# Sharing a weight copy between VectorE and GpSimd, and placing two ScalarE output copies ahead of a sigmoid, in a fused retention and mixture-of-adapters kernel

## The chip, the cores and the metric

The kernel runs on one core of a Trainium2 chip. The metric is the device time of one execution in microseconds (us). A core has TensorE (PE, matmuls; PEld is its weight load), VectorE (DVE), ScalarE (ACT), GpSimd (POOL) and SyncE (SP, which here issues most DMA transfers). Each engine runs its own instructions in program order and waits on semaphores for the others.

## The reference

A retention layer (attention with a decay instead of a softmax) feeds a mixture of low-rank adapters. With B = 8, H = 8, S = 576 and head size 64:

```python
scores = scale * np.matmul(q, k.transpose(0, 1, 3, 2))
Dmat = np.where(rel >= 0, gamma[:, None, None] ** rel[None, :, :], 0.0)   # rel = i - j
ret = scores * Dmat[None]
attn_out = np.matmul(ret, v)
x = attn_out.transpose(0, 2, 1, 3).reshape(B * S, H * D)                  # 4608 x 512

logits = x @ w_gate                                                       # 8 adapters
topk = the 2 adapters with the largest logits;  w = softmax over these two
delta = sum over the two of  w * ((x @ A[e]) @ B[e])                      # rank 16
out = x + delta
```

## The kernel before, in words

The decay factorizes, so the sequence is cut in chunks of 128 positions (four full ones and a last one of 64). A *unit* is one chunk of two batch entries, with all 8 heads; a *quad* is one chunk of four entries, and it is loaded as a whole: q, k and v by one transfer each from SP (`issue`, line 225). There are 18 units; units 0 to 3 are the first chunk.

For each unit t the kernel goes through stages, all called by hand in the loop at the end of the function:
- `stage_T`: q and k are transposed on TensorE into PSUM (tiles pqT, pkT) and copied to SBUF (qT, kT). For each name there are two banks g = 0 and 1. With `shared=True` the copy of g = 1 is VectorE's and that of g = 0 ScalarE's; otherwise both are ScalarE's, but for the q of units 0 and 1, which are VectorE's.
- `stage_S`: scores (ps) per head pair, multiplied by the mask on VectorE (rt). `scale_k` on GpSimd multiplies k by decay factors; `stage_U` forms the state update (pu).
- `stage_Q` and `stage_R`: the old state and the masked scores give the retention output (px), which VectorE scales into xT, one tile per batch entry g.
- `stage_Z`: for both g, TensorE multiplies xT by AW[g], which holds the adapters' A (columns 0 to 127, `ER`) and the gate (columns 128 to 135), giving pz. Then VectorE copies the logits (lg), takes their maxima (m) and a bias ns. `stage_V` is the sigmoid of the routing on ScalarE (sg), and `stage_W` forms the routing weights (cm) and the weighted low-rank activations (zc) on VectorE.
- `stage_B` transposes xT back into the output banks po[cc], `stage_X` transposes zc (pzt, then zT on ScalarE), and `stage_Y` adds zT times B (`Bcat`) to po (`mm_Y`), copies the four pieces of po to SBUF (osb, `copy_Y`: cc chooses the bank, g the half of it) and stores them from SP (`store_Y`).

Units have their heads on the partitions in one order for g = 0 and with the partition halves exchanged for g = 1. So AW is needed twice: AW[0], and AW[1], which is AW[0] with its two halves of 64 partitions exchanged. `place_A` puts A into AW[0] by matmuls (pa) and four ScalarE copies; a GpSimd transfer (line 679) brings the gate. Lines 693 and 694 are the two GpSimd copies from AW[0] to AW[1], and line 695 is the GpSimd transfer of B.

What sets the order: TensorE, VectorE and ScalarE instructions are recorded through `mm`, `vec` and `act` (lines 81, 84, 87), which chain every instruction of an engine to the one before it, so each of these engines runs in the order in which the stages are called; `chain("pool", ...)` does the same for a few GpSimd instructions. So all TensorE matmuls have line 81, all chained VectorE operations line 84 and all ScalarE operations line 87; tiles, not lines, tell them apart. The eight PSUM banks are handed out from a first-in first-out list: `bank` takes the oldest free one, `done` appends a bank when its last reader has been recorded. A tile that gets a bank waits for the last reader of the tile that had it before. In this way the two banks of unit 3's pkT are one that the pzt of unit 0 left, and the bank of po[0] of unit 0.

The stretch that the diff touches is the body of `t == 0`: units 0 and 1, with the transposes of units 2 and 3 already begun. `stage_Y(0, copies=("act", "dve"))` gives the two pieces of bank cc = 0 to ScalarE and those of cc = 1 to VectorE.

Of the kernel before, what the change touches and what calls it, by code (L numbers as in the profile page):

```python
# [18 lines left out]
def kernel(  # L19
# [15 lines left out]
    ER = E * R  # L35
# [21 lines left out]
    for hp in range(HP):  # L57
        for ho in range(2):
            g = gam[2 * hp + ho]
# [13 lines left out]
    def chain(eng, i):  # L73

        i = getattr(i, "ins", i)
        if eng in queued:
            tc.add_manual_dep(i, queued[eng].name, order, reason="program order")
        queued[eng] = i
# [4 lines left out]
    def vec(fn, **kw):  # L83
        chain("dve", getattr(nc.vector, fn)(**kw))  # L84
# [31 lines left out]
    gp = nc.gpsimd  # L116
# [3 lines left out]
    for base in (0, -L):  # L120
        gp.affine_select(
            out=id64, in_=id64, compare_op=ALU.not_equal, fill=1.0, base=base,
# [129 lines left out]
    def rows(g):  # L252
        return slice(64 * g, 64 * g + 64)
# [17 lines left out]
    def stage_T(t, names=("qT", "kT"), shared=False):  # L271

        s = st.setdefault(t, {})
        for nm in names:
            src = nat[units[t]][0 if nm == "qT" else 1]
            dst = s[nm] = wk.tile([128, 2, HP, C], FP32, tag=nm, name=nm, bufs=4 if nm == "qT" else 2)
            ps = [bank([128, HP, 2, L], f"p{nm}") for _ in range(2)]
            for hp in range(HP):
                for b in range(2):
                    for g in range(2):  # L280
                        mm(
                            ps[g][:, hp, b, :],
                            lhsT=src[rows(g), b, 2 * hp : 2 * hp + 2, :],
                            rhs=id64[rows(g), :],
                            is_transpose=True,
                            start=True,
                            stop=True,
                        )
            for g in range(2):
                if is_full(t):  # L290
                    o = dst[:, :, :, rows(g)].rearrange("p b a i -> p a b i")
                else:
                    o = dst[:, g].rearrange("p a (b i) -> p a b i", b=2)
                if t < 2 and nm == "qT" or shared and g == 1:
                    vec("tensor_copy", out=o, in_=ps[g])
                else:
                    act("copy", out=o, in_=ps[g])
            done(*ps)
# [214 lines left out]
    def stage_Z(t, gs=BOTH):  # L513

        s = st[t]
        n = len(gs)
        pz = bank([128, n, ER + E], "pz")
        for y, g in enumerate(gs):
            for dt in range(HP):
                mm(  # L520
                    pz[:, y, :],
                    lhsT=s["xT"][g][:, dt, :],
                    rhs=AW[g][:, dt, :],
                    start=(dt == 0),
                    stop=(dt == HP - 1),
                    skip_group_check=True,
                )
        m8 = mo.tile([128, n, E], FP32, tag=f"m8{n}", name="m8")
        ns = mo.tile([128, n], FP32, tag=f"ns{n}", name="ns")
        lg = mo.tile([128, n, E], FP32, tag=f"lg{n}", name="lg")  # L530
        if n == 2:
            vec("tensor_copy", out=lg, in_=pz[:, :, ER : ER + E])
        else:
            lg = pz[:, :, ER : ER + E]
        for y in range(n):
            vec("max", out=m8[:, y, :], in_=lg[:, y, :])
        vec(
            "scalar_tensor_tensor",
            out=ns, in0=m8[:, :, 0], scalar=-1.0, in1=m8[:, :, 1],
            op0=ALU.mult, op1=ALU.subtract,  # L540
        )
        s[("route", gs)] = lg, m8, ns, pz

    def stage_V(t, gs=BOTH):
        s = st[t]
        n = len(gs)
        lg, m8, ns, pz = s[("route", gs)]
        sg = mo.tile([128, n, E], FP32, tag=f"sg{n}", name="sg")
        for y in range(n):
            act(  # L550
                "activation",
                out=sg[:, y, :], in_=lg[:, y, :], func=AFT.Sigmoid,
                bias=ns[:, y : y + 1], scale=2.0,
            )
        s[("route", gs)] += (sg,)
# [26 lines left out]
    def mm_Y(t, gs=BOTH):  # L582

        s = st[t]
        if gs[0] == 0:
            s["osb"] = outp.tile([128, 2, HP, 2, Dh], FP32, tag="osb", name="osb")
        bv = Bcat.rearrange("p (a o d) -> p a o d", a=HP, o=2)
        for cc in range(2):
            for g in gs:
                mm(  # L590
                    s["po"][(cc, g)],
                    lhsT=s["zT"][g],
                    rhs=bv[:, :, cc ^ g, :],
                    start=False,
                    stop=True,
                    skip_group_check=True,
                )
# [26 lines left out]
    def stage_Y(t, gs=BOTH, copies=("act", "act")):  # L624

        mm_Y(t, gs)
        for cc in range(2):
            for g in gs:
                copy_Y(t, cc, g, copies[cc])
        store_Y(t, gs)  # L630
# [40 lines left out]
    for t in range(NU):  # L671
        if units[t][2] == 0:
            issue(quads.index(units[t][:2]) + 2, (0, 1, 2) if t <= LATE else (0,))
        if t == 0:
            spin(10)
            first_T()
            scale_k(0)
            fill_pick(3)
            gp.dma_start(
                out=AW[0][:, :, ER : ER + E], in_=moe_w_gate.rearrange("(t p) e -> p t e", p=128)  # L680
            )
            for ho in range(2):
                act("copy", out=asc[1][rows(ho)], in_=asc[0][rows(1 - ho)])
            act(
                "copy", out=gdec.rearrange("p a b d -> p a (b d)"),
                in_=gde.unsqueeze(2).broadcast_to((128, HP, 2 * Dh)),
            )
            stage_S(0)
            stage_U(0)
            stage_Q(0)  # L690
            stage_R(0)
            place_A()
            for ho in range(2):
                chain("pool", gp.tensor_copy(out=AW[1][rows(ho)], in_=AW[0][rows(1 - ho)]))
            chain("pool", gp.dma_start(out=Bcat, in_=moe_B.rearrange("e r d -> (e r) d")))
            stage_T(1, ("qT",))
            stage_T(1, ("kT",), shared=True)
            scale_k(1)
            stage_Z(0)
            stage_S(1)  # L700
            stage_W(0)
            stage_U(1)
            stage_Q(1)
            stage_R(1)
            stage_T(2, ("qT",))
            stage_B(0)
            stage_X([0])
            stage_Z(1)
            stage_V(1)
            stage_Y(0, copies=("act", "dve"))  # L710
            stage_T(2, ("kT",), shared=True)
            stage_T(3)
            scale_k(2)
            scale_k(3)
            stage_S(2)
            stage_W(1)
            stage_S(3)
            for u in (2, 3):
                stage_U(u)
                stage_Q(u)  # L720
                stage_R(u)
            late_T(4)
            for ho in range(2):
                gp.tensor_tensor(
                    out=maskh[ho], in0=trih.unsqueeze(1).broadcast_to((128, HP, L)),
                    in1=heads(1, ho, L), op=ALU.mult,
                )
            continue
        if t < 4 or units[t][2] or not is_full(t):
            continue  # L730

        before, near = [u for u in (t - 4, t - 3) if u > 0], (t - 2, t - 1)
        here = (t, t + 1)
        for u in here:
            for b, nm in enumerate(("qT", "kT")):
                stage_S(u, (b,))
                if t > LATE:
                    stage_T(u + 2, (nm,))
            if t > LATE:
                scale_k(u + 2)  # L740
        for u in before:
            stage_B(u)
        stage_X(before)
        stage_Z(near[0])
        stage_V(near[0])
        for u in before:
            stage_Y(u)
        stage_Z(near[1])
        stage_V(near[1])
        if t > LATE:  # L750
            issue(t // 2 + 2, (1,))
        if units[t][0] > 0:
            for u in here:
                stage_Q(u)
        for u in near:
            stage_W(u)
        for u in here:
            if t > LATE and u == here[1]:
                issue(t // 2 + 2, (2,))
            stage_U(u)  # L760
            if units[t][0] == 0:
                stage_Q(u)
            stage_R(u)
        if t <= LATE:
            late_T(t + 2)
# [80 lines left out]
```

## Time and profile before

| | |
|---|---|
| median of 4 runs | 184.32 us (183.04 to 186.62) |
| the profiled execution's own time | 183.96 us |
| its span, first to last instruction | 182.3 us |
| granted TensorE clock, mean | 0.991 |
| busy: PE, DVE, ACT, POOL | 173.9, 114.7, 67.0, 58.6 us |
| HBM traffic | 28.91 MB read, 9.44 MB written |

The profile is one execution as the hardware profiler took it. Times count from the start of the span. A timeline row reads: start, duration (from the first to the end of the last of a merged group), engine, line, operation, output tile, input tiles, shape, count, and in brackets how long the engine had been idle before it and what ended that wait. The chain of waits is followed back from the last instruction, at each step to what released it. A wait on several semaphores is put down to the one that came last by the profile. Matmuls are pipelined, so the duration of one is longer than the distance between two.

### The profile page before, as it was taken

The page shows a single profiled execution, that of the slowest core. Times are in us where ns is not written, and L with a number is a line of the kernel's source. Part 1 is how long each engine was busy: PE and PEld are TensorE (multiplying, and loading weights), DVE is VectorE, ACT ScalarE, POOL GpSimd, SP SyncE. Part 2 cuts the span into 40 slices and gives each one's busy share as a digit, 9 for nine tenths or more (in the row PEclk, how much of TensorE's full clock was granted, in tenths as well). Part 3 has the DMA queues.
Part 4 walks back from the last instruction along what each step waited for, and adds up shares of the span by engine and source line. Part 5 has one row for each costly group of instructions (what it writes and reads, how often), then busy time and mean ns, then how long its engine had stood idle before and what let it go on. Part 6 is the DMA issues. An engine that isn't in the chain of part 4 may idle for free.

```text
span 182.3 us, 8097 instructions
## 1 busy us (share of the span) xinstructions
PE 173.9 (95%) x3606; PEld 162.6 (89%) x3606; DVE 114.7 (63%) x293; ACT 67.0 (37%) x180; POOL 58.6 (32%) x69
## 2 busy tenths in 40 slices
PE   7897999999999999999999999999999999999980
PEld 2596989999999999999999999999999999999970
DVE  3594856988567836866267816792488446557471
ACT  3512127043313243197602753075505460031461
POOL 8865208044026500687022710444050003200000
PEclk9999999999999999999999999999999999999996
DMA  6998979999798898769898989997691041014055
GB/s 138 278 229 210 318 211 297 274 288 278 213 284 247 245 320 233 217 192 294 230 327 286 297 248 313 262 201 154 236 203 29 4 177 60 4 57 182 7 229 230
DMA packets 53219, 38.74 MB, mean 213 GB/s; under 512 B 26928, under 2 KB 48576, under 8 KB 53184
## 3 DMA queue, kind: packets, MB, share of 16 engines
q1 hardware_dynamic: 50784, 37.49, 71.3%
q10 hardware_dynamic: 2224, 0.58, 1.5%
q8 instruction: 28, 0.46, 1.1%
q0 software_dynamic: 176, 0.15, 0.5%
q14 instruction: 7, 0.06, 0.1%
HBM read 28.91 MB, written 9.44 MB: 210 GB/s over the span
## 4 chain that ended last, share of the span: by engine, by line
PE 91%; DMA 3%; DVE 2%; ACT 1%; ACTq 1%; issue 0%
PE px L81 24%; PE pz L81 19%; PE ps L81 17%; PE pu L81 9%; PE po L81 9%; PE pkT L81 5%; PE pqT L81 5%; DMA k<-in_k_dram 3%; PE pzt L81 2%; PE pe L81 1%; DVE qT L84 1%; ACT osb L87 1%; PE pa L81 1%; ACT sg L87 0%; ACTq L225 0%
## 5 line engine op out<-in xcount | busy, mean ns | idle before, releaser
L84 DVE TENSOR_TENSOR rt<-ps,mask 128x512 f32<-128x512 f32 x64 | 40.3, 685 | 8.9 <-PE ps L81 8.0
L264 POOL TENSOR_TENSOR k<-k,pack 128x512 f32<-128x512 f32 x32 | 32.6, 1044 | 25.1 <-PE pkT L81 18.4
L423 POOL TENSOR_TENSOR P<-pn,gdec 128x512 f32<-128x512 f32 x12 | 15.3, 1277 | 68.2 <-DVE pn L84 64.0
L81 PE MATMUL pz<-AW,xT 128*128 128x136 f32 x288 | 37.1, 282 | 0.0
L81 PEld LDWEIGHTS pz<-AW,xT 128*128 128x128 f32 x288 | 34.6, 190 | 0.2
L81 PE MATMUL ps<-qT,kT 64*128 64x128 f32 x512 | 34.1, 278 | 0.0
L81 PEld LDWEIGHTS ps<-qT,kT 64*128 64x128 f32 x512 | 30.7, 188 | 1.2 <-issue 0.8
L81 PE MATMUL px<-rt,v 128*64 128x128 f32 x512 | 30.7, 273 | 0.0
L87 ACT COPY qT<-pqT 128x512 f32<-128x512 f32 (+1 forms) x33 | 16.8, 568 | 31.3 <-PE pqT L81 31.3
L81 PEld LDWEIGHTS px<-rt,v 128*64 128x64 f32 x512 | 27.7, 137 | 0.0
L84 DVE TENSOR_TENSOR xT<-px,asc 128x512 f32<-128x512 f32 x36 | 24.4, 689 | 4.0 <-PE px L81 2.6
L87 ACT COPY kT<-pkT 128x512 f32<-128x512 f32 x29 | 16.0, 600 | 27.4 <-PE pkT L81 18.7
L84 DVE COPY lg<-pz 128x16 f32<-128x16 f32 x17 | 3.0, 175 | 32.5 <-PE pz L81 32.5
L87 ACT COPY osb<-po 128x256 f32<-128x256 f32 x59 | 17.3, 388 | 2.7 <-PE po L81 2.0
L81 PE MATMUL pu<-v,k 128*64 128x64 f32 x512 | 18.1, 224 | 0.0
L81 PEld LDWEIGHTS pu<-v,k 128*64 128x64 f32 x512 | 16.6, 138 | 1.4 <-issue 1.0
L87 ACT ACTIVATE sg<-lg,ns 128x8 f32<-128x8 f32 x34 | 8.4, 294 | 23.3 <-DVE ns L84 22.9
L81 PE MATMUL pkT<-id,k 64*128 64x64 f32 x288 | 12.7, 225 | 1.8 <-DVE qT L84 1.3
L81 PE MATMUL px<-qT,P 64*64 64x128 f32 (+1 forms) x512 | 14.2, 259 | 0.0
L81 PEld LDWEIGHTS pkT<-id,k 64*128 64x128 f32 x288 | 11.2, 139 | 2.9 <-DVE qT L84 1.5
L84 DVE TENSOR_TENSOR pn<-pu,P 128x512 f32<-128x512 f32 x12 | 8.3, 692 | 8.3 <-PE pu L81 8.3
L81 PEld LDWEIGHTS px<-qT,P 64*64 64x64 f32 x512 | 12.6, 133 | 0.9
(59 smaller groups left out, 149.6 us busy)
## 6 DMA issues: line engine op xcount, KB each, us to landing
out_dram<-osb SPq DMA_DIRECT2D x36, 256.0 KB, 3.9
v<-in_v_dram SPq DMA_DIRECT2D x4, 512.0 KB, 7.2
q<-in_q_dram SPq DMA_DIRECT2D x3, 512.0 KB, 5.3
k<-in_k_dram SPq DMA_DIRECT2D x3, 512.0 KB, 7.6
q<-in_q_dram SPq DMA_DIRECT2D x2, 256.0 KB, 4.2
k<-in_k_dram ACTq DMA_DIRECT2D x2, 256.0 KB, 4.8
Arow<-in_moe_A_dram SPq DMA_DIRECT2D x1, 256.0 KB, 6.8
Bcat<-in_moe_B_dram POOLq DMA_DIRECT2D x1, 128.0 KB, 4.7
```

The costliest lines, as they stand in the source:

```text
L81: chain("pe", nc.tensor.matmul(*args, **kw))
L84: chain("dve", getattr(nc.vector, fn)(**kw))
L87: chain("act", getattr(nc.scalar, fn)(**kw))
L264: gp.tensor_tensor(out=kk[:, b], in0=kk[:, b], in1=gv[:, 0].unsqueeze(2).broadcast_to((128, H, Dh)), op=ALU.mult,)
L423: nc.gpsimd.tensor_tensor(out=Pt, in0=pn, in1=gdec, op=ALU.mult)
```

## The change

The two parts lie in the body of `t == 0`. The first gives the A columns of one half of AW[1] to VectorE, behind the q copies of unit 1, and leaves GpSimd that half's gate columns (64 partitions x 4 x 8). The second takes `stage_Y(0)` apart and calls it ahead of `stage_V(1)`: ScalarE's two osb copies of unit 0 come before unit 1's sigmoid pair. The order of TensorE's and of SP's instructions stays as it was; VectorE's order gains one copy, GpSimd's second AW copy is smaller, and ScalarE's order differs in those four instructions.

```diff
             place_A()
-            for ho in range(2):
-                chain("pool", gp.tensor_copy(out=AW[1][rows(ho)], in_=AW[0][rows(1 - ho)]))
+            chain("pool", gp.tensor_copy(out=AW[1][rows(0)], in_=AW[0][rows(1)]))
+            chain("pool", gp.tensor_copy(out=AW[1][rows(1), :, ER:], in_=AW[0][rows(0), :, ER:]))
             chain("pool", gp.dma_start(out=Bcat, in_=moe_B.rearrange("e r d -> (e r) d")))
             stage_T(1, ("qT",))
+            vec("tensor_copy", out=AW[1][rows(1), :, 0:ER], in_=AW[0][rows(0), :, 0:ER])
             stage_T(1, ("kT",), shared=True)
             scale_k(1)
             stage_Z(0)
...
             stage_B(0)
             stage_X([0])
             stage_Z(1)
+            mm_Y(0)
+            for cc, eng in enumerate(("act", "dve")):
+                for g in range(2):
+                    copy_Y(0, cc, g, eng)
+            store_Y(0)
             stage_V(1)
-            stage_Y(0, copies=("act", "dve"))
             stage_T(2, ("kT",), shared=True)
             stage_T(3)
             scale_k(2)
```

## The prediction

> **What bounds the kernel now.** I read the page's busy shares first, then its 40 slices, then the whole chain of waits in order of time, and then, for the two places that the diff touches (13 to 20 us and 25 to 31 us), the timeline of each engine.
>
> ```profile
> PE 173.9 (95%) x3606; PEld 162.6 (89%) x3606; DVE 114.7 (63%) x293; ACT 67.0 (37%) x180; POOL 58.6 (32%) x69
> PE   7897999999999999999999999999999999999980
> PEclk9999999999999999999999999999999999999996
> ```
>
> TensorE is busy 95% of the span at the full granted clock until the last slice. An edit to another engine can only pay where TensorE stands still, and all its idle time is 182.3 - 173.9 = 8.4 us, start and tail included. So the first question is which of its idle time the edits can reach. The chain of waits around the two places:
>
> ```profile
> 13.81 0.69 PE pqT L81 x16
> 14.50 1.29 DVE qT L84 x2
> 15.79 0.01 issue
> 15.80 0.71 PE pkT L81 x16
> 16.51 2.05 PE pz L81 x16
> 18.56 1.99 PE ps L81 x32
> ...
> 27.36 0.49 ACT sg L87 x2
> 27.85 0.54 ACT osb L87 x2
> 28.39 0.04 issue
> 28.44 0.71 PE pkT L81 x15
> 29.15 3.78 PE ps L81 x64
> ```
>
> There are two holes. The first, 14.50 to 15.80, is put down to VectorE's qT copies. That name cannot be right: pkT reads k and writes the two banks that the xT products left, and those products were done before the qT copies began. The other thing pkT needs is the second k load, issued at 7.92 us; the trace's answer for k between 7.5 and 9.5 us is
>
> ```profile
> DMA to landing us min/median/max: 7.7/7.7/7.7
> ```
>
> and 7.92 + 7.7 = 15.6 us, just ahead of pkT's first weight load at 15.77. The hole is a transfer's, and the diff does not touch that transfer. The second hole, at 28.4, is ScalarE's. The weight loads and ScalarE's own row there:
>
> ```profile
> 28.01 0.14 PEld L81 LDWEIGHTS pkT<-id,k 64*128 64x128 f32 x1
> 28.43 0.57 PEld L81 LDWEIGHTS pkT<-id,k 64*128 64x128 f32 x15 [0.28 <-ACT osb L87]
> 28.92 2.70 PEld L81 LDWEIGHTS ps<-qT,kT 64*128 64x128 f32 x44
> ```
> ```profile
> 27.36 0.49 ACT L87 ACTIVATE sg<-lg,ns 128x8 f32<-128x8 f32 x2 [1.96 <-DVE ns L84]
> 27.76 0.62 ACT L87 COPY osb<-po 128x256 f32<-128x256 f32 x2
> 28.28 0.59 ACT L87 COPY kT<-pkT 128x512 f32<-128x512 f32 x1
> 28.75 1.09 ACT L87 COPY qT<-pqT 128x512 f32<-128x512 f32 x2
> 29.71 1.11 ACT L87 COPY kT<-pkT 128x512 f32<-128x512 f32 x2
> ```
>
> Unit 3's kT transposes write two banks. The first was free; the second is the bank of the first output's half cc = 0, which ScalarE frees with its second osb copy at 27.76 + 0.62 = 28.38. In the timeline these 16 transposes take 1.08 us where the 16 of unit 2 just before take 0.71: the hole costs 0.37 us. ScalarE stood idle for 1.96 us ahead of the sigmoid, in program order, while the osb copies behind it had their data.
>
> **Part 1, the weight copies.** Before: two GpSimd copies of 64x544 (15.43 to 16.74; 636 ns each). After: one of them stays; GpSimd's second shrinks to 64x32; VectorE takes 64x512, behind its qT copies (end 14.49 + 1.29 = 15.78) and ahead of its kT copy (16.55).
>
> GpSimd's small copy: the nearest rows are 64x64 at 239 ns and a 128x1 memset at 100 ns; I take 0.24, so GpSimd ends near 16.07 + 0.24 = 16.3 instead of 16.74. VectorE's copy: no row copies SBUF to SBUF there. Its copy of 512 elements from PSUM takes 0.69, its memset of 256 words 0.27; bounds 0.27 and 0.69. I take 0.69, the row with the same element count, which ends at 15.78 + 0.69 = 16.47, inside the 0.78 us for which VectorE idles before kT.
>
> Who reads the result: stage_Z(0), whose first eight matmuls use AW[0] and whose last eight use AW[1]. It starts at 16.44, behind the transposes of unit 1, and half of its 2.05 us brings it to AW[1] near 17.4. The copies were there at 16.74, 0.7 us early; now they are there at 16.5. TensorE waited for neither in the trace and gains nothing. The same holds for what is queued behind on GpSimd: the Bcat load moves from 16.69 to about 16.3 (it landed 4.7 us after its issue, 21.4, and its first reader runs at 26.48), and scale_k(1) from 17.35 to about 17.0 (its reader, stage_U(1), starts at 20.48). On VectorE the kT copy and the routing's lg wait for TensorE in any case (0.78 and 1.35 us idle before them). SP's queue keeps its order. Term: 0. The cover is about 0.7 us of early arrival; past it, each 0.1 us of lateness costs 0.1 us.
>
> [...]
>
> [...] With the three copies strictly one after another, GpSimd 15.43 to 16.07, VectorE to 16.76, GpSimd to 17.00: still 0.4 us ahead of 17.4. The kT copy would then run 16.76 to 17.45, against its reader S(1) at 18.49. So the first part costs 0 to its upper bound as well. Nothing excludes a small loss from a slower copy than any row shows; that is the slower rival below.
>
> **Part 2, the osb copies ahead of the sigmoid.** The matmuls of po and their order are unchanged: stage_Y's matmuls already stood ahead of unit 2's transposes on TensorE. ScalarE's first osb copy waits for two of the four po matmuls; these start 0.11 us apart from 26.48 and the last ends at 27.08, so the second ends at 26.86. ScalarE has been free since 25.40. The two copies run 26.90 to 27.52 (0.62 for the pair). The sigmoid's bias ns is ready at 27.17 + 0.16 = 27.33, so the sigmoid pair now starts at 27.5 instead of 27.36 and ends at about 27.98 instead of 27.85: 0.13 later. Its first reader, cm of stage_W(1), ran at 32.52: hidden by 4.5 us. VectorE's own osb copies wait for the last po matmul as before. The output's two stores are issued from SP in the same place of its queue, at 35.88 behind a v load, so copies that end 0.9 us earlier do not move them.
>
> Behind the sigmoid on ScalarE, unit 2's kT copy starts 0.4 us earlier, since ScalarE now works in what was idle time: about 27.88 to 28.47 instead of 28.28 to 28.87. The copies after it follow, and the last kT copy of unit 3 ends near 30.82 - 0.39 = 30.43.
>
> TensorE: the bank is free at 27.52, before the transposes reach it at 28.07, so 0.37 us of stall go. What is late next? S(2), which began its weight loads at 28.92, needs kT of unit 2 from both engines. ScalarE's half is there at 28.47. VectorE's half is not moved by the diff: 27.91 + 0.68 = 28.59, and with the 0.05 us that lay between ScalarE's half (28.87) and S(2) it can start at 28.64. The gain is 28.92 - 28.64 = 0.28 us; bounds 0 and 0.37. I take 0.28, because VectorE's chain lg, m, ns, osb, osb, kT is unchanged row by row.
>
> Does it last? S(3) begins half of the two units' 3.78 us after S(2), at about 30.55, and ScalarE's last kT copy ends at 30.43, so it does not hold it. From 30.11 to 40.5 VectorE works without a break, but that run starts with a product that waits 1.52 us for S(2), so it shifts along. The third quad's k load, issued at 28.24 with 9.1 us to landing, is there at 37.3, and its transposes would come at 38.37 - 0.28 = 38.09. After 41 us the transfers land microseconds ahead. So 0.28 us should reach the end.
>
> **Sum.** The profiled execution took 183.96 us around a span of 182.3: 183.96 - 0 - 0.28 = 183.68, span 182.0. It lies 0.36 us under the median of the four runs, 184.32; against that median the forecast is 184.32 - 0.28 = 184.0 us. A measurement of this kernel can tell about 1% (1.8 us) from no change, so the verdict should be "the same".
>
> **Rivals.**
> - *The gain is given back (184.3).* Place: the third quad's k load. It lands 0.8 us before the earlier transposes. DMA runs at 0.94 of its engines in that stretch, and a landing 0.8 to 1.1 us later than in this execution takes all of it. For it: the four runs differ by 2%. Against it: the profiled margin.
> - *Slower: the weight copies run late.* Mechanism: VectorE and GpSimd slow each other on their concurrent copies. It decides from an end past 17.4. If all three are serial and each takes twice its row: 15.43 + 1.27 + 1.38 + 0.48 = 18.56, 1.2 us late, and 184.32 + 1.2 - 0.28 = 185.2. For it: the three are now on two engines at one moment. Against it: before, GpSimd's copies took 634 and 637 ns although VectorE's qT copy ran beside the first.
> - *The edit does nothing (184.3).* It would be so if the osb copies, now in front, had to wait for po past 27.36. The po matmuls end by 27.08, and Bcat has landed 5 us before: little for it.
>
> **How the numbers follow.** The forecast, a gain of 0.2 to 0.37: 60%. Gain given back or never there: 24%. Late copies: 8%. Something that no row shows: 8%, either way. Nearly all of the first two, and a late copy of 1.2 us, lie within 1%. So: within 1% 0.86, slower 0.08, faster 0.06. The range reaches up to the late copies, 185.2. Below, no part gives more than 0.37, but the runs of one kernel scatter more than that: I reach to the fastest run of before, 183.0. The likeliest case's own range is 183.9 to 184.1 around that median.
>
> **What would show it.** Right: in the changed profile the wait of pkT's weight load on ACT osb near 28.4 is gone; osb stands at about 26.9 and the sigmoid after it; the transposes of unit 3 take about 0.7 us; S(2) starts at about 28.64, then waiting for VectorE's kT; the hole at 14.5 to 15.8 is as it was. Wrong: pz waits for VectorE or GpSimd near 17.4; or pkT at 38 waits for its load; or an earlier S(2) without a shorter span.

## The result and the profile after

| | before | after |
|---|---|---|
| median of the runs, us | 184.41 (182.93 to 188.09) | 184.54 (182.65 to 187.23) |
| the profiled execution, us | 183.96 | 182.65 |
| its span, us | 182.3 | 181.0 |

The ratio after to before is 0.9998 (95% interval 0.9978 to 1.0018): no difference that this measurement can tell. (The ratio leaves out executions more than 1.5% above the kernel's fastest, so it is not quite the ratio of the two medians.) A second measurement of the same kernel on another occasion, among the experiments below, gave 0.9942 (0.9901 to 0.9984). The forecast was 183.68/183.96 = 0.9985: well inside the first interval, just above the second, whose own ratio would be a gain of 1.1 us. The two intervals share only 0.9978 to 0.9984. The times alone do not settle whether 0.28 us were won; for that the traces are needed.

The page of the changed kernel, its span and busy times:

```profile
span 181.0 us, 8099 instructions
PE 173.9 (96%) x3606; PEld 162.4 (90%) x3606; DVE 115.2 (64%) x294; ACT 67.1 (37%) x180; POOL 58.1 (32%) x69
```

TensorE does the same 173.9 us of work in a span 1.3 us shorter. Most of that is not the change's. The chain of waits (start, length, what):

```profile
7.70 7.04 DMA k<-in_k_dram
14.73 0.14 issue
14.87 0.71 PE pkT L81 x16
15.58 2.05 PE pz L81 x16
17.63 1.99 PE ps L81 x32
...
26.80 0.51 PE pqT L81 x16
27.31 0.51 PE pkT L81 x16
27.81 1.14 PE ps L81 x16
```

Unit 1's transposes now begin at 14.87 instead of 15.80, and here the chain names the releaser: the k load, landed at 14.73. In this execution it simply landed 0.93 us earlier. So hole and load go together, and an execution's time contains this load's luck. The second place, in the weight loads of TensorE and then in ScalarE's rows:

```profile
27.09 0.59 PEld L81 LDWEIGHTS pkT<-id,k 64*128 64x128 f32 x16
27.78 3.68 PEld L81 LDWEIGHTS ps<-qT,kT 64*128 64x128 f32 x64
```
```profile
25.98 0.65 ACT L87 COPY osb<-po 128x256 f32<-128x256 f32 x2 [1.50 <-PE po L81]
26.51 0.51 ACT L87 ACTIVATE sg<-lg,ns 128x8 f32<-128x8 f32 x2
26.90 0.59 ACT L87 COPY kT<-pkT 128x512 f32<-128x512 f32 x1
```

Unit 3's transposes are one group of 16 again, with no wait on osb in it; osb runs while ScalarE would wait for ns, and the sigmoid follows. To take the first load's luck out, count from the first weight load of S(1) to the first weight load of later groups (S(t) and U(t) are `stage_S` and `stage_U` of unit t):

| S(1) to, us | S(2) | U(2) | S(4) | third quad's k load lands before its reader by |
|---|---|---|---|---|
| before | 10.43 | 14.37 | 22.14 | 0.99 |
| after | 10.22 | 14.02 | 21.85 | 0.28 |

So 0.21 us are won at S(2), 0.35 at U(2) and 0.29 at S(4). From S(1) to the end of the span it is 163.4 instead of 163.8 us.

### The profile page after: what moved, and what is told of

Its sections match the earlier page's. It is cut to its first block, busy times and chain, and to the rows that moved or that the text cites. A ratio compares the mean times of both kernels' runs of the same rounds, so it can differ in the third digit from the quotient of the medians.

```text
span 181.0 us, 8099 instructions
## 1 busy us (share of the span) xinstructions
PE 173.9 (96%) x3606; PEld 162.4 (90%) x3606; DVE 115.2 (64%) x294; ACT 67.1 (37%) x180; POOL 58.1 (32%) x69
## 4 chain that ended last, share of the span: by engine, by line
PE 83%; issue 5%; DMA 4%; SPq 4%; ACT 2%; DVE 1%; ACTq 0%
PE px L81 21%; PE pz L81 19%; PE ps L81 15%; PE po L81 9%; PE pu L81 7%; PE pkT L81 4%; PE pqT L81 4%; DMA k<-in_k_dram 4%; SPq L171 2%; PE pzt L81 2%; SPq L225 2%; PE pe L81 1%; ACT kT L87 1%; ACT qT L87 1%; ACT osb L87 0%
## 5 line engine op out<-in xcount | busy, mean ns | idle before, releaser
L87 ACT COPY kT<-pkT 128x512 f32<-128x512 f32 x29 | 16.0, 600 | 26.5 <-PE pkT L81 17.7
L81 PE MATMUL px<-qT,P 64*64 64x128 f32 (+1 forms) x512 | 14.1, 259 | 0.0
L87 ACT COPY zT<-pzt 128x512 f16<-128x512 f16 (+2 forms) x12 | 5.8, 483 | 18.9 <-PE pzt L81 18.9
```

The lines of the kernel that those rows point to most:

```text
L81: chain("pe", nc.tensor.matmul(*args, **kw))
L87: chain("act", getattr(nc.scalar, fn)(**kw))
```

## The experiments

The table gives those whose stretches can be compared, all counted as above; the others follow in the text. "pkT to S(1)" counts from unit 1's k transposes and is the stretch in which the weight copies are used; the two landings are those of unit 1's k load and the third quad's.

| kernel | ratio to before (95%) | first landing | third quad's | pkT to S(1) | S(1) to S(2) | to U(2) | to S(4) |
|---|---|---|---|---|---|---|---|
| before | | 15.66 | 37.38 | 2.72 | 10.43 | 14.37 | 22.14 |
| full change | 0.9998 (0.9978 to 1.0018) | 14.73 | 36.80 | 2.72 | 10.22 | 14.02 | 21.85 |
| full again | 0.9942 (0.9901 to 0.9984) | 14.51 | 36.83 | 2.78 | 10.22 | 14.02 | 21.86 |
| part 1 alone | 1.0002 (0.9968 to 1.0036) | 15.15 | 39.13 | 2.74 | 10.49 | 14.42 | 23.49 |
| part 2 alone | 0.9976 (0.9944 to 1.0008) | 14.34 | 36.80 | 2.73 | 10.32 | 14.12 | 21.99 |
| late osb, half | 0.9993 (0.9944 to 1.0041) | 14.91 | 38.10 | 2.73 | 11.00 | 14.84 | 22.72 |
| slow copies | 1.0115 (1.0070 to 1.0159) | 15.87 | 38.83 | 3.78 | 10.21 | 14.02 | 21.84 |
| q first, full | 0.9951 (0.9905 to 0.9997) | 14.50 | 37.65 | 2.73 | 10.21 | 14.01 | 22.09 |
| both q first | 0.9996 (0.9949 to 1.0043) | 14.32 | 38.24 | 3.16 | 10.22 | 14.02 | 22.42 |

**Part 2 alone.** The hunk of the diff around `mm_Y(0)`, without the one around `place_A()`.

> Only the output copies move ahead of the sigmoid; the weight copies are as before. Theory (TensorE-bound, the bank wait at 28.4 us goes, 0.28 us reach the end): the wait of the second pkT weight load on osb is gone; measured from the first weight load of unit 1's pkT (which follows the k load's landing), S(2) comes 0.2 to 0.28 us earlier than before, S(3) up to 0.38, everything after 41 us 0.28; ratio near 0.9985, hardly to be told from 1. Rival 1 (the gain is given back at the third quad's k load): the same up to 31 us, but unit 4's pkT waits for its load, and the distance from unit 1's pkT to S(4) is that of before. Rival 2 (the weight copies cost what the output copies bring): a ratio clearly below that of the full change, about 0.997.

The wait on osb is gone. S(2) comes 0.11 earlier than before, U(2) 0.25, S(4) 0.15. That is the gain of the full change less 0.1, and at S(2) less than the expected 0.2: between 17 and 23 us TensorE lost 0.1 us in this execution, which has nothing to do with osb, and at 36.9 the third quad's load (landed 36.80) left no margin. Ratio 0.9976 with an interval that holds 1: as expected, not to be told from it, so it does not decide rival 2 either.

**Part 1 alone.** The hunk around `place_A()`, without the other.

> Only the weight copies are shared; the output copies are as before. Theory: no distance between TensorE's groups changes by more than 0.03 us; pz starts when pkT ends and does not wait for VectorE or GpSimd; ratio 1.000. Rival 2: pz's second half waits for VectorE's copy, 0.1 us or more; ratio about 1.0015 or above.

Nothing is won and nothing lost up to U(2) beyond 0.06, and the ratio, with a third of a per cent either way, shows no cost. But its profile shows the first rival at work, by a transfer that neither part touches (TensorE's rows):

```profile
36.31 1.70 PE L81 MATMUL px<-rt,v 128*64 128x128 f32 x28
39.26 0.71 PE L81 MATMUL pkT<-id,k 64*128 64x64 f32 x16 [1.26 <-DMA k<-in_k_dram]
```

The third quad's k load landed at 39.13 and TensorE stood still for 1.26 us. In such an execution any gain ahead of it is given back. What moves this landing is mostly when SP issues the load: over all profiles between 27.09 (the copies made to meet) and 29.71 us (slow copies), here at 29.70; from issue to landing it is 8.7 to 9.5 us everywhere.

**The output copies late.** On the kernel before, ScalarE's two copies go behind three other copies of ScalarE's:

```diff
             stage_V(1)
-            stage_Y(0, copies=("act", "dve"))
+            mm_Y(0)
+            for g in range(2):
+                copy_Y(0, 1, g, "dve")
+            done(*st[0]["banks"].values())
+            st[0]["banks"] = {}
             stage_T(2, ("kT",), shared=True)
-            stage_T(3)
+            stage_T(3, ("qT",))
+            for g in range(2):
+                copy_Y(0, 0, g, "act")
+            store_Y(0)
+            stage_T(3, ("kT",))
```

> The opposite of part 2, made large: on the kernel before, ScalarE's two output copies of unit 0 go behind the copies of unit 2's kT and unit 3's qT. The bank of unit 3's second pkT half is then free near 29.9 instead of 28.4. Theory (what is lost or won at 28 us reaches the end): the wait grows from 0.36 to about 1.85 us, S(2) comes 1.5 later, S(3) 1.3 to 1.5 later, and the time rises by about 1.35 us, ratio 1.007. Rival 1 (time at 28 us is absorbed by the wait for the third quad's load at 37 to 38 us): S(2) as late, but S(4) less than 0.7 us late; ratio 1.000 to 1.003.

Ratio 1.0081 (1.0042 to 1.0120): a loss reaches the end, and rival 1's upper 1.003 is excluded. That its size, 1.5 us, lies near the 1.35 forecast is partly luck. Of the eight executions behind the ratio four had a mean granted clock of 0.985 to 0.989, below that of all 25 of the kernel before (0.991 to 1.000), and lie 1.6 to 3.0 us above its median of 184.12; the other four, at 0.993 to 0.995, lie about 1.0 above it. The clock's share was not in the forecast. The profile is of an execution (188.29) longer than the kernel's median (185.76) and has a further loss: the second quad's k load, landing at 26.92, held unit 2's transposes for 1.02 us. What it shows of the clock is told at the end.

**Half as late.** The same, but with the two copies directly behind unit 2's kT copy.

> On the kernel before, ScalarE's two output copies of unit 0 go behind unit 2's kT copy only. The bank is then free about 0.5 us later than before. Theory: the wait of the second pkT weight load grows from 0.36 to about 0.85 us and the groups up to 37 us shift by 0.5; that reaches the end except where the third quad's k load is the later one. At such a small hole the granted clock stays at 1.00 (in the run with the late copies it fell to 0.50 behind holes of 1.02 and 1.65 us). Ratio 1.001 to 1.003. Rival 1 (time at 28 us does not matter): 1.000.

```profile
27.39 0.14 PEld L81 LDWEIGHTS pkT<-id,k 64*128 64x128 f32 x1
28.32 0.51 PEld L81 LDWEIGHTS pkT<-id,k 64*128 64x128 f32 x14 [0.79 <-ACT osb L87]
```

From 27.39 to 28.32 the second load comes 0.93 us behind the first, where it was 0.42 before (28.01 to 28.43): 0.5 more, and S(2), U(2) and S(4) come 0.57, 0.47 and 0.58 later, 0.1 of it lost between 17 and 23 us as in part 2 alone. In the trace the loss arrives; the ratio, 0.9993 with half a per cent either way, is inconclusive. The granted clock did not fall behind this hole: 63 weight loads of the scores took 3.65 us from 28.82 on, where in the run with the late copies, at a clock of 0.50, 63 took 6.13.

**The weight copies made slow.** The full change with VectorE's weight copy recorded four times (`for _ in range(4)`).

> The full change with VectorE's weight copy written four times over (three are superfluous): it ends about 1.2 us later, near 17.5 instead of 16.3 us. Theory (cover, and beyond it each 0.1 us costs 0.1): pz's second half waits for VectorE. By the runs so far it is wanted 1.7 us after the k load lands, so the wait is about 1.1 us where that load lands at 14.7 and 0.2 where it lands at 15.7; up to 1.5 at 14.3. From unit 1's pkT to S(1) that much is added to 2.7 us, and all later groups shift by it, as long as the third quad's load is there. Ratio 1.000 to 1.006. Rival (the copies are hidden whatever they take, for VectorE and TensorE have other work): no wait, ratio 0.998 to 1.000.

The rival is out: TensorE waits, as the theory said, but for longer: pkT to S(1) grows by 1.06 us where the expectation, with the load at 15.87, gave less than 0.2, and the ratio is 1.0115 instead of at most 1.006. The copies themselves were mis-sized. Rows of VectorE (the third copy, at 16.92, is like the second) and of GpSimd (start, length):

```profile
15.81 0.62 DVE L84 COPY AW<-AW 64x512 f32<-64x512 f32 x1
16.46 0.42 DVE L84 COPY AW<-AW 64x512 f32<-64x512 f32 x1
17.38 1.15 DVE L84 COPY AW<-AW 64x512 f32<-64x512 f32 x1
17.11 1.14 POOL L264 TENSOR_TENSOR k<-k,pack 128x512 f32<-128x512 f32 x1
```

The same copy takes 0.42 us alone, 0.62 when GpSimd's copy is still running as it comes (to 16.15), and 1.15 when scale_k is running (17.11 to 18.24). The fourth ended at 18.5 instead of near 17.5. The ratio is 2.1 us, twice what this execution lost. An estimate from its rows fits that: the copies' end does not follow the load, so with the load at 14.73, as in the profile after, the same end would have cost 1.06 + 1.14 = 2.2 us.

**The copies made to meet.** VectorE's copy ahead of its q copies, GpSimd's first one cut to the A columns:

```diff
-            chain("pool", gp.tensor_copy(out=AW[1][rows(0)], in_=AW[0][rows(1)]))
-            chain("pool", gp.tensor_copy(out=AW[1][rows(1), :, ER:], in_=AW[0][rows(0), :, ER:]))
+            chain("pool", gp.tensor_copy(out=AW[1][rows(0), :, 0:ER], in_=AW[0][rows(1), :, 0:ER]))
+            for ho in range(2):
+                chain("pool", gp.tensor_copy(out=AW[1][rows(ho), :, ER:], in_=AW[0][rows(1 - ho), :, ER:]))
             chain("pool", gp.dma_start(out=Bcat, in_=moe_B.rearrange("e r d -> (e r) d")))
+            vec("tensor_copy", out=AW[1][rows(1), :, 0:ER], in_=AW[0][rows(0), :, 0:ER])
             stage_T(1, ("qT",))
-            vec("tensor_copy", out=AW[1][rows(1), :, 0:ER], in_=AW[0][rows(0), :, 0:ER])
```

> The full change, but with VectorE's and GpSimd's weight copies made to start together: GpSimd's first copy takes only the A columns (64x512), so that it needs only ScalarE's copies (about 14.6 us), the two gate pieces follow in small copies, and VectorE's copy stands ahead of its q copies and needs the same. Theory without exclusion: both run side by side from about 14.6, VectorE's for 0.42 and GpSimd's for about 0.62 us. [...]

```profile
14.71 0.42 DVE L84 COPY AW<-AW 64x512 f32<-64x512 f32 x1 [1.18 <-ACT AW L87]
14.81 0.79 POOL L693 COPY AW<-AW 64x512 f32<-64x512 f32 x1 [2.02 <-ACT AW L87]
```

VectorE's copy came first and kept its 0.42 us; GpSimd's took 0.79, where its larger 64x544 copy takes 0.64. So the two did not run side by side undisturbed: GpSimd's copy took 0.15 us longer than the larger one, and TensorE, whose pz wants the last gate piece, lost 0.08 (pkT to S(1) is 2.80). One execution, 182.81 us.

**Room for the late load.** In `late_T`, for unit 4 alone, the q transposes come ahead of the k transposes: `for nm in ("qT", "kT") if t == 4 else ("kT", "qT")`.

> The full change with one exchange more: unit 4's q transposes come ahead of its k transposes, whose load is the last to land (36.3 to 39.1 us in the profiles so far; unit 4's pkT followed it by 0.1 us in two of them). Theory (the gain at 28 us is given back in those executions where this load is late): TensorE has 0.5 us of work more before it needs the load, so where the load is late up to 0.5 us is gained, elsewhere nothing; ratio to the kernel before 0.996 to 0.999, no wait of pkT at 37 to 39 us of more than what the load exceeds 0.5 us by. Rival (the load is hardly ever the bound): as the full change, 0.998 to 1.000.

Ratio 0.9951 (0.9905 to 0.9997), just under the expected range; the full change alone gave 0.9998 and 0.9942, so the exchange's share cannot be read from it. In the profile the load landed at 37.65 and TensorE waited 0.22 us for it behind the q transposes; without them it would have stood still from 36.85.

**The first hole filled too.** The same, with the gate loaded from ScalarE's queue at the start, VectorE's weight copy ahead of its q copies, `stage_Z(0)` ahead of unit 1's k transposes and `stage_B(0)` behind them.

> The same, and the first hole is filled: the gate is loaded early from ScalarE's queue, VectorE's weight copy stands ahead of its q copies, and stage_Z(0) comes ahead of unit 1's k transposes, with stage_B(0) behind them. TensorE then has 2.0 us of work before it needs unit 1's k load (14.3 to 15.7 us). Theory: no wait for that load; S(1) starts at about 17.7 whatever the load does, with 0.5 us of later work already done; 0.1 to 1.2 us gained up to 37 us, and there the third quad's load takes part of it back. Ratio 0.994 to 0.998. Rival (the loads bound the first 38 us in any case): pkT of unit 4 waits for its load in most executions and the ratio is that of q_first.

Ratio 0.9990 (0.9941 to 1.0039), short of the forecast. The first hole went (pkT at 16.92 follows pz at once), but S(1) began at 18.54 instead of 17.7: pz waited 0.27 us for GpSimd's weight copy, and S(1) 0.41 us; the trace names the sigmoid for that, but VectorE's kT copy, which S(1) needs, ended just before, at 18.39. And two later loads were waited for all the same (TensorE's rows):

```profile
39.00 0.71 PE L81 MATMUL pkT<-id,k 64*128 64x64 f32 x16 [0.69 <-DMA k<-in_k_dram]
```
```profile
82.95 0.72 PE L81 MATMUL pkT<-id,k 64*128 64x64 f32 x16 [2.00 <-DMA k<-in_k_dram]
```

The rival's mechanism holds here: what is won ahead of 38 us meets the third quad's load, and what is left of it meets the sixth quad's, which landed at 82.81.

**The exchange with and without the change, on one chip.** Three variants and the full change again.

> The kernel before with only the exchange at unit 4 (its q transposes ahead of its k transposes); neither part of the change. Theory (the change's 0.28 us are real, and where the third quad's load is late they are given back unless the exchange makes room): ratio 0.997 to 1.000, and on this chip 0.1 to 0.2% above that of the full change with the exchange. Rival (the exchange alone made the earlier run's 0.995, the change adds nothing): the same ratio as with the change. In the profile: the wait of the second pkT weight load at 28 us for osb, 0.36 us, is there.

> The full change with the exchange, once more, beside the others on one chip. Theory: ratio 0.995 to 0.999, the distance from unit 1's pkT to S(2) 12.94 us as in its first profile, no wait of pkT at 37 to 39 us unless its load lands more than 23.1 us after unit 1's pkT began.

> The full change, and both units' q transposes (4 and 5) ahead of the k transposes: 1.0 us of TensorE work ahead of the third quad's k load instead of 0.5. Theory: no wait for that load below a distance of 23.6 us; but S(4) then waits 0.1 to 0.3 us for unit 4's kT copies, which are no longer covered; ratio within 0.002 of that of the single exchange.

> The full change itself, once more, for its profile: it shows how much of the 0.28 us is left in another execution. Theory: from unit 1's pkT to S(2) 12.94 us and to U(2) 16.74 us, as in its first profile, and to S(4) 24.57 us unless the third quad's k load lands more than 22.1 us after unit 1's pkT began; then later by the excess. Ratio 0.997 to 1.001.

Ratios: the exchange alone 0.9987 (0.9932 to 1.0043), with the change 0.9937 (0.9890 to 0.9984), with both q's first 0.9996 (0.9949 to 1.0043), the change without the exchange 0.9942 (0.9901 to 0.9984). The last three lie outside what was expected of them, though their intervals reach into it. The order of the first two fits a real gain by the change, but their intervals overlap, and their distance, 0.5%, is three times the 0.28 us of the traces, so it proves nothing of that size. The exchange adds nothing that can be seen: no version is shown to beat the full change.

The traces are plainer. In the profile of the exchange alone the wait on osb is there, and S(2) and U(2) come 10.43 and 14.37 us behind S(1), as before. In that of the full change S(1) to S(4) is 21.86, as in its first one. The profile of the exchange with the change lost 0.9 us between 17 and 24 us, 0.67 of it in one wait that the trace puts down to issue, so its S(2) came 13.82 and not 12.94 us behind pkT: that expectation failed.

With both q's first the third quad's load came late (38.24), and S(4) then waited 0.44 us for ScalarE's kT copies, where 0.1 to 0.3 were expected. Its profile also showed a cost of part 1 (rows of VectorE, then of the weight loads):

```profile
14.61 1.29 DVE L84 COPY qT<-pqT 128x512 f32<-128x512 f32 x2 [1.03 <-PE pqT L81]
15.93 0.42 DVE L84 COPY AW<-AW 64x512 f32<-64x512 f32 x1
```
```profile
15.10 0.99 PEld L81 LDWEIGHTS pz<-AW,xT 128*128 128x128 f32 x8
16.47 0.99 PEld L81 LDWEIGHTS pz<-AW,xT 128*128 128x128 f32 x8 [0.38 <-issue]
```

The k load landed at 14.32, so pz began at 15.10 and wanted AW[1] at about 16.0; VectorE's copy, behind the qT copies, ended at 16.35. pkT to S(1) is 3.16 instead of 2.72. With GpSimd's two copies and a load as early (part 2 alone, 14.34) it is 2.73.

## Why the prediction was right, point by point

- *The first hole is the load's.* Right, and shown: in all 13 profiles that keep this order the weight loads of unit 1's pkT begin 0.10 to 0.11 us behind the landing, wherever that falls (15.66, 14.73, 15.15), and the trace names the load where the hole is shorter.
- *Part 1 at 0.* Right as far as the times can tell; two of its terms were off. VectorE's copy was taken at 0.69 and takes 0.42; it is not like the copy from PSUM of the same size, which takes 0.69. The cover was mis-sized: "about 0.7 us of early arrival" took TensorE's start at 16.44 as given, but that start follows the load, while VectorE's copy follows its q copies. At the earlier landing of the profile after, the copy ended at 16.32 for a weight load at 16.43, and TensorE waited for it in two others (0.06 in full again, 0.44 with both q's first). What counts is how soon unit 1's k transposes follow its q transposes: after 0.94 and 0.56 us in these two, after 0.99 or more in the profiles with part 1 as made and no such wait. So part 1 gains nothing and costs 0 to 0.4 us, as the load falls.
- *"Past it, each 0.1 us of lateness costs 0.1 us".* Shown as far as S(4) by the slow copies, whose delay went into pkT to S(1) and from there unchanged into S(4) (21.84 behind S(1), as in the full change).
- *Part 2 at 0.28.* Right: 0.29 at S(4). That the total fits so closely is partly luck, for its steps differ from those of the forecast: the wait on osb went (0.36); S(2) won 0.21 instead of 0.28, since it began 0.12 us behind VectorE's kT copy (27.66 to 27.78) where 0.05 was taken; U(2) won 0.35, because ScalarE's last kT copy, which S(3) had followed by 0.05 us before, no longer holds it; and 0.06 went again at S(4).
- *Does it last?* The loss experiment shows that time at 28 us reaches the end on the whole. But the margin of the third quad's load, forecast at 0.8, was 0.28 in the profile after and 0.1, that is just in time or late, in seven others (part 1 alone, part 2 alone, half as late, q first, full again, both q first, the first hole filled too); in part 1 alone TensorE lost 1.26 us. And "after 41 us the transfers land microseconds ahead" was misread. The sixth quad's k load landed at 79.54 in the profile before, 1.10 us ahead of its first weight load at 80.64, and at 79.31 in the profile after, 0.12 us ahead. Three other profiles waited for it: 1.02 us (both q first), 1.52 (the exchange with the change) and 2.00 (the first hole filled too). "The gain is given back" got 24% and describes a good part of the executions, at either load. How many, 14 profiles cannot say.
- *The verdict.* "Within 1%" was safe because the gain is 0.15% of the time. That it cannot be seen in the times is due to single executions, which move by more than the change does: the first landing lies between 14.28 and 15.87, the third quad's between 36.25 and 39.13, the sixth quad's load makes TensorE wait or not, and TensorE has waits that the trace puts down to nothing but issue (0.70 us at 79.43 in full again, 1.17 at 94.51 in slow copies).

## What to carry to other kernels

Find out first whose hole it is: where a wait's named releaser had nothing to give, look for the landing that falls on its end; a change to the engine named there moves nothing (here the stall ended 0.1 us behind the landing, wherever that fell). A gain in front of a transfer that lands just in time is worth its size only in the executions where the transfer is early, so compare distances between groups of the busy engine, not spans, and read the margin of every load up to the end, not of the next one alone. And a cover read from one profile is two independent chains' distance: ask what each of its ends follows before spending it.

## What the runs showed of the hardware

*VectorE and GpSimd copies.* Where VectorE's copy from SBUF to SBUF met a GpSimd operation on SBUF, the one that came later took longer: VectorE's 0.42 us became 0.62 and 1.15 (slow copies), and GpSimd's copies took 0.79 instead of about 0.6 (the copies made to meet; the 0.6 is estimated from the 0.64 of 64x544) and 0.83 instead of 0.63 (64x544, the first hole filled too). In all four the later one ended about 0.13 us sooner than if it had begun only when the other ended: 0.62 instead of 0.76, 1.15 instead of 1.28, 0.79 instead of about 0.92, 0.83 instead of 0.96. In the profile after, GpSimd's copies had all but ended when VectorE's began (15.92 for GpSimd, 15.90 for VectorE), and nothing was lost; in the execution of the slow copies the first of the four, which is the change's own, took the 0.62.

*The granted clock.* A hole in TensorE's work can cost more than itself. With the output copies late, holes of 1.02 and 1.65 us stood 1.3 us apart (rows of TensorE, then the stretches: length, busy times, granted clock, DMA):

```profile
28.08 0.22 PE L81 MATMUL pkT<-id,k 64*128 64x64 f32 x1
29.96 1.11 PE L81 MATMUL pkT<-id,k 64*128 64x64 f32 x15 [1.65 <-ACT osb L87]
30.77 6.32 PE L81 MATMUL ps<-qT,kT 64*128 64x128 f32 x64
```
```profile
29.10:35.90 6.80, 5.94 (x63) 5.94 (x65) 2.66 (x6) 1.88 (x5) 2.77 (x3) 0.50 0.97 266
```

The 64 score matmuls took 6.32 us instead of 4.00. The exchange alone showed the same behind one hole of 1.85 us (14.1 to 15.9 us), where the first load was late; its stretch by the same columns:

```profile
16.30:19.70 3.40, 3.40 (x25) 3.28 (x21) 0.69 (x1) 0.58 (x1) 3.29 (x5) 0.50 0.95 255
```

Single holes of 1.26, 1.34 and 1.56 us (part 1 alone, before, slow copies) left the clock at 1.00, and so did the hole of 2.00 us at 80.95 (the first hole filled too): the length of a hole alone does not decide. (For the last this follows from the mean granted clock of its execution, 0.997: one stretch of 3.4 us at 0.50 in the span of 184.8 would alone have made it 0.991.) The half clock lasted 3.4 us behind the one hole of 1.85 and 6.8 us behind the two of the late copies.

At the end of the program the clock stayed at 1.00 behind the last matmul for 1.0 us in the profile before (178.14 to 179.1) and for 2.9 us in the profile after (176.83 to 179.7), and was 0.50 from there to the end of the span. So the time since TensorE's last work does not decide either; what does stays open.
